# Splitting the second-layer weight sums and the activation split in two, and fetching the Wb tiles three steps ahead, in a fused attention and two-MoE kernel

## The chip, the cores and the metric

One core of a Trainium2 chip. The metric is the device time of one execution in microseconds. The kernel before has a median of 1530.12 us over 3 runs (1529.88 to 1532.5).

## The reference

Three stages follow one another; all tensors hold B = 8 batches of S = 576 tokens, 4608 tokens in all, and 512 model columns (8 heads of 64):

```python
p_packed = sm_attn(p, k, v)                  # 32 packed queries per head
x = sm_attn(q, p_packed, p_packed)           # then heads side by side: 4608 x 512
h = x @ w_in                                 # 512 x 2048
P = a[0] + a[1]*h + a[2]*h**2 + a[3]*h**3
Q = 1 + |b[0]|*|h| + |b[1]|*h**2
x = (P / (Q + 1e-6)) @ w_out                 # 2048 x 512
h = x @ moe2_w_in
out = (max(h, 0) + alpha*min(h, 0)) @ moe2_w_out
```

The weights come as 64-bit floats and are turned into 32-bit floats on the chip.

## The kernel before

**The three parts.** Until about 177 us the attention runs, and PE folds its second product with `w_in` into a matrix Wb for each batch (stored to DRAM, `wb_d`). From 177 to about 829 us the first MoE runs; it is the part in which the change lies. After that the second MoE runs as seven block products by sums of weight blocks (lines 1067 and 1075), which were made ready during the first MoE.

**The steps of the first MoE.** The loop at L843 takes 72 steps and three more (`LAG` = 3). Step g is one chunk c of 512 tokens and one f of the eight 256-column slices of the hidden layer. Nine chunks take pieces ("shares") of two batches' visits, 192 and 320 tokens, 256 and 256, or 320 and 192. In step g PE runs 24 matmuls of `emit_L1(g)` (L600: h = a2 times a Wb tile) and then 24 of `emit_L2(g - 3)` (L680: into `acc`). Each product is made of three passes over pairs of a high and a low half, which is why every operand is split: a copy rounded to the high half on ACT, and the rest by a subtraction on POOL. h lies in PSUM and has two buffers.

**The other engines in a step.** ACT: Abs (L642), two Identity (L643, L644), the high half of the activation of the step before (L626), the reciprocal square root (L657) and its square (L658). POOL: q times r (L645), the low half (L627). DVE: two operations on v (L650, L651) and three that end the step (L663 to L665, the last to read h). At f = 2 two finished accumulators go out through `yo` (L616, L614) and six stores (L621).

**The Wb tiles.** A visit is the use of one batch's Wb; `VISITS` lists ten, eight batches and two of them a second time. Tile n is visit n // 8, slice n % 8. It is first used at step n - 8, as the second share of a chunk, and again at step n. `next_wb(g)` at the end of step g first brings the tile fetched in the step before to its slot (`split_wb`): for a first visit ACT and POOL split it (L520, L521); for the second visits (tiles 48 to 55 and 72 to 79) the two halves, which `keep_wb` (L526) had stored, are read straight to the slot by one DMA (L518). Then it fetches tile g + 16 (`fetch_wb`, L511). So a tile is fetched 16 steps ahead of its number, and split or read back 15 ahead.

**The activations.** At f = 1 the next chunk's a2 is loaded (L495), and at f = 3, at the end of the step, `split_a2` splits it whole (L501 on ACT, L502 on POOL).

**The second layer's weights.** `w2_step(s, part)` is called at three places of a step ("start", "dve" and "end"); with n, half = divmod(s - 9, 2) it takes a 64-bit weight tile n through two steps. Its magnitude is made on ACT from the high words (L84) and the low words (L85), bounded on DVE (L89), joined (L92) and signed (L95). Each pair of tiles then yields four sums on POOL (L714), is stored by two DMAs (`w2_store`, L719), and its buffers, three in all under the tag `s4`, are loaded anew (`w2_load`, L707). So four steps make one cycle:

- n even, half 0 (f = 1 and 5): start: store the pair before, load tile n + 1; DVE: bound n;
- n even, half 1 (f = 2 and 6): DVE: join and sign n; end: magnitude of n + 1;
- n odd, half 0 (f = 3 and 7): start: load n + 1; DVE: bound n;
- n odd, half 1 (f = 4 and 0): DVE: join and sign n; end: magnitude of n + 1, and the four sums of the pair.

All DMAs named here are issued by SP, in the order of the program; one that waits keeps back those behind it.

Of the kernel before, what the change touches and what calls it, by code (L numbers as in the profile page):

```python
# [11 lines left out]
F32 = mybir.dt.float32  # L12
F32R = mybir.dt.float32r
I32 = mybir.dt.int32
I64 = mybir.dt.int64
U8 = mybir.dt.uint8
AF = mybir.ActivationFunctionType
ALU = mybir.AluOpType
# [10 lines left out]
def attention_then_two_moes(ctx, tc, qT, kT, v, pT, w_in, w_out, ab, w2_in, w2_out, alpha, out):  # L29
    nc = tc.nc  # L30
    mm = nc.tensor.matmul
    act = nc.scalar.activation
    dve = nc.vector
    pool = nc.gpsimd
# [7 lines left out]
    CH = 512  # L42
    NCH = NT // CH
    NF = 16
    NP = NF // 2
    LAST = B // 2 - 1
    VISITS = (0, 1, 2, 3, 4, 5, 0, 6, 7, 3)
# [31 lines left out]
    REBIAS = 2.0 ** -112  # L79
    HIGH_R = float(np.array(0x0FEFFFFF, np.int32).view(np.float32))  # L80

    def magnitude(w, st):
        words = st.bitcast(I32).rearrange("p (n t) -> p n t", t=2)
        act(w, words[:, :, 1].bitcast(F32), AF.Abs, scale=REBIAS)  # L84
        act(words[:, :, 0], st.bitcast(U8).rearrange("p (n t) -> p n t", t=8)[:, :, 3], AF.Copy, scale=1.0 / 32, bias=-31.0 / 64)  # L85
        return words

    def bounded(w):
        dve.tensor_scalar(w, w, 0.0, HIGH_R, op0=ALU.max, op1=ALU.min)  # L89
# [18 lines left out]
    def s2_tile():  # L108
        return gp.tile([128, 512], F32, tag="s2", name="s2", bufs=3)
# [99 lines left out]
    for h in range(4):  # L209
        o = 64 * (h % 2)  # L210
# [267 lines left out]
    spx = open_pool("spx", bufs=2, side="right")  # L478
    a2_t = {}

    chunks, taken = [], [0] * B
    for c in range(NCH):
        o, now = 0, []
        for i, n in enumerate(SHARES[c % 3]):
            b = VISITS[c + i]
# [9 lines left out]
            nc.sync.dma_start(out=st[:, :, o:o + n], in_=a2_d[b][:, :, t:t + n])  # L495
        a2_t[c] = st

    def split_a2(c):
        st = a2_t[c]
        t = spx.tile([128, 2, 2, CH], F32R, tag="a2t", name="a2t")  # L500
        act(t[:, 0], st, AF.Copy)  # L501
        pool.tensor_tensor(t[:, 1], st, t[:, 0], op=ALU.subtract)  # L502
        a2_t[c] = t

    def fetch_wb(n):
        v, f = divmod(n, NP)
        if v > VISITS.index(VISITS[v]):
            wb_q.append((v, f, None))
            return
        wb_q.append((v, f, s2_tile().rearrange("p (k f) -> p k f", k=2)))  # L510
        nc.sync.dma_start(out=wb_q[-1][2], in_=wb_d[VISITS[v]][:, 256 * f:256 * f + 256].rearrange("(k p) f -> p k f", p=128))  # L511
# [16 lines left out]
    w2_st, w2_mag = {}, {}  # L528

    def w2_abs(n):  # L530
        if n < 2 * NF:
            st = w2_st[n]
            if st.dtype == I64:
                w2_mag[n] = s2_tile()
                magnitude(w2_mag[n], st)
# [20 lines left out]
    for c in DRAIN.split():  # L556
        if c == "W":
            store_Wb()
            emit_Wb(nwb[0])
            nwb[0] += 1  # L560
        elif c == "L":
            load_a2(0)
        elif c == "l":
            split_a2(0)
        elif c == "o":
            load_late(len(late_st))
            w2_st[len(late_st) - 1 - LATE] = late_st[-1]
        elif c == "a":
            w2_abs(magged[0] - LATE)
            magged[0] += 1  # L570
        elif c == "c":
            w2_range(-LATE)
            w2_bits(-LATE)
        else:
            {"A": emit_a2, "B": store_a2, "S": emit_s2, "E": emit_exp2, "Q": load_q}[c[0]](NQ - int(c[1]))
# [8 lines left out]
    NG = NCH * NP  # L584
# [46 lines left out]
    def emit_E1(s):  # L631


        late_step(s, "start")
        w2_step(s, "start")
        if s < NG:
            h = hps.pop(s)
            r_ = spa.tile([128, 2, CH], F32, tag="r_", name="r_", bufs=1)
            q_ = spa.tile([128, 2, CH], F32, tag="q_", name="q_", bufs=2)
            v_ = vs[s] = spa.tile([128, 2, CH], F32, tag="v_", name="v_", bufs=2)  # L640
            now[s] = h, r_, q_, v_
            act(r_, h, AF.Abs)  # L642
            act(q_, r_, AF.Identity, scale=b1, bias=b0)  # L643
            act(v_, h, AF.Identity, scale=a3, bias=a2c)  # L644
            pool.tensor_tensor(q_, q_, r_, op=ALU.mult)  # L645
        if 1 <= s <= NG:
            emit_hi(s - 1)
        late_step(s, "middle")
        if s < NG:
            dve.tensor_tensor(v_, v_, h, op=ALU.mult)  # L650
            dve.scalar_tensor_tensor(v_, in0=v_, scalar=a1c, in1=h, op0=ALU.add, op1=ALU.mult)  # L651
# [47 lines left out]
    def w2_load(n):  # L699
        if n < 2 * NF:  # L700
            if n < 0:
                load_late(n + NF - EARLY)
                w2_st[n] = late_st[-1]
                return
            src, view = w2_source(n)
            st = w2_st[n] = gp.tile([128, 512 if src.dtype == I64 else 1024], src.dtype, tag="s4", name="s4", bufs=3)
            nc.sync.dma_start(out=view(st[:, 0:512]), in_=src)  # L707

    def w2_sums(n):

        a11, a22, s1, s2, s3, s4 = piece(n - 1, 0), piece(n, 1), piece(n - 1, 2), piece(n - 1, 3), piece(n, 2), piece(n, 3)
        a12, a21 = (piece(n - 1, 1), piece(n, 0))[::1 if n < NF else -1]
        for o, a, b, op in ((s1, a21, a22, ALU.add), (s3, a11, a21, ALU.subtract), (s2, s1, a11, ALU.subtract), (s4, a12, s2, ALU.subtract)):
            pool.tensor_tensor(o, a, b, op=op)  # L714

    def w2_store(n):
        y, r = divmod(n // 2, HF)
        for h in range(2):
            nc.sync.dma_start(out=wq_d[y][r // 2][:, 4 * h:4 * h + 4, r % 2, :],  # L719
                              in_=w2_st.pop(n - 1 + h).bitcast(F32).rearrange("p (i f) -> p i f", i=4))  # L720
# [23 lines left out]

    def w2_step(s, part):


        n, half = divmod(s - 9, 2)
        if part == "start" and not half:
            if n % 2 == 0 and 2 <= n <= 2 * NF:  # L750
                w2_store(n - 1)
            if n >= -1:
                w2_load(n + 1)
        elif part == "dve":
            if 0 <= n < 2 * NF:
                (w2_bits if half else w2_range)(n)
        elif part == "end" and half:
            if n >= -1:
                w2_abs(n + 1)
            if n % 2 and 0 <= n < 2 * NF:  # L760
                w2_sums(n)

# [47 lines left out]
    def split_y(s, i, src):  # L812
# [15 lines left out]
                dve.tensor_tensor(lo, x, hi, op=ALU.subtract)  # L828
        return rest

    def next_wb(g):

        while wb_q:
            split_wb()
        if g + 2 * NP < len(VISITS) * NP:
            fetch_wb(g + 2 * NP)
        c, f = divmod(g, NP)
        for i in range(3) if g == 0 else (g + 2,) if g + 2 < NP else ():
            keep_wb(0, i)
        if c == 2:  # L840
            keep_wb(3, f)

    for g in range(NG + LAG):  # L843
        if g == NG:
            close_pool("spx")
            spy = open_pool("spy", bufs=1, side="right")
            load_y(0)
        if g < NG:
            c, f = divmod(g, NP)
            if f == 1 and c + 1 < NCH:  # L850
                load_a2(c + 1)
            emit_L1(g)
            for _ in range(FILL[g] if g < len(FILL) else 0):
                emit_Wb(nwb[0])
                nwb[0] += 1
        if g == LAG - 1:
            close_pool("psw2")
            close_pool("psw")
            psa = open_pool("psa", bufs=1, space=PSUM, side="right")
        emit_E1(g)  # L860
        if g >= LAG:
            emit_L2(g - LAG)
        emit_E2(g)
        store_Wb()
        if g < NG:
            next_wb(g)
            if f == 3 and c + 1 < NCH:
                split_a2(c + 1)
        d = g - NG
        if d == -1:  # L870
            pool.tensor_scalar(nalpha, alpha_sb, -1.0, None, op0=ALU.mult)
            for n, st in enumerate((gp.tile([128, 2, CH], F32, tag="ast", name="wst", bufs=1),
                                    spa.tile([128, 2, CH], F32, tag="q_", name="wst", bufs=2))):
                for x in range(2):
                    w_load(2 * n + x, st[:, x])
        elif d >= 0:
            if d == 0:
                for n, tag in ((2, "v_"), (3, "q_")):
                    st = spa.tile([128, 2, CH], F32, tag=tag, name="wst", bufs=2)
                    for x in range(2):  # L880
                        w_load(2 * n + x, st[:, x])
            for u in range(4 * d, min(4 * d + 4, SOON)):
                w_split(u, dve)()
            if d:
                split_y(0, d - 1, y_block(0, d - 1, 0))()
# [155 lines left out]
    for u in range(len(units) + 2):  # L1041
        if u < len(units):
            s, y, i, n = units[u]
# [11 lines left out]
            w = ws.pop(u)  # L1055
# [6 lines left out]
            if y == 0:  # L1062
                for g in range(2):
                    q = 0
                    for x, z in PASSES:
                        for k in range(2):
                            mm(ps[:, g, 0:m], w[:, g, x, 128 * k:128 * k + 128], ysp[s, i](z, k),  # L1067
                               start=not onto and q == 0, stop=q == 5, skip_group_check=again)
                            q += 1
            else:  # L1070
                t = vsp.pop(u)
                for g in range(2):
                    for d in range(2):
                        for q, (x, z) in enumerate(PASSES):
                            mm(ps[:, d, 0:m], w[:, g, x, 128 * d:128 * d + 128], t[:, z, g, 0:m],  # L1075
                               start=not onto and n == 0 and g == 0 and q == 0, stop=n == 3 and g == 1 and q == 2,
# [61 lines left out]
```

## Time and profile before

| | |
|---|---|
| median of 3 runs | 1530.12 us |
| profiled execution | 1529.2 us, span 1527.4 us |
| PE busy | 1460.6 us (96%) |
| DVE busy | 1297.4 us (85%) |
| ACT busy | 1030.2 us (67%) |
| POOL busy | 570.4 us (37%) |

Shares are of the whole span. All times in rows are microseconds from the span's start, unless marked ns. A releaser in brackets (`[2.01 <-POOL q L645]`) is the idle time just before an instruction and what ended it. PE's matmuls are pipelined and their ends are modelled, so that the distance of two starts says more than a duration. The clock is the share of its full speed that TensorE was granted.

### The profile page before, as it was taken

The numbers are of one execution on the slowest core, as the hardware profiler recorded it, in microseconds if no ns is written. First come the engines' busy times: TensorE is split into PE (matmuls) and PEld (weight loads), VectorE is DVE, ScalarE is ACT, GpSimd is POOL, SyncE is SP. The second block draws the span as 40 slices with busy tenths as digits, with TensorE's granted clock in tenths as the row PEclk, the third lists the DMA queues.
The fourth block names the chain that finished last, engine by engine and source line by source line (L and its number), as shares of the span: only waits on it lengthen the run. The fifth ranks groups of instructions, "written<-read, shape, count | busy, mean of one in ns | idle before, by whom it ended". The sixth has DMA issues, their size and how long they took to land.

```text
span 1527.4 us, 20922 instructions
## 1 busy us (share of the span) xinstructions
PE 1460.6 (96%) x7712; PEld 1204.5 (79%) x7712; DVE 1297.4 (85%) x1412; ACT 1030.2 (67%) x1194; POOL 570.4 (37%) x354
## 2 busy tenths in 40 slices
PE   4798878999999999999999999999999999999998
PEld 2444477888888888888888877888888888888898
DVE  5988789898889999899999799859966996599586
ACT  4456588988988888888886586447434743474363
POOL 3132288788787778877664610000000000000000
PEclk9899989999999999999999999999999999999999
DMA  9999944236433632424435977997567656765694
GB/s 353 342 315 295 318 154 130 67 110 200 156 111 97 211 107 84 125 97 145 145 97 194 329 241 252 376 379 273 202 209 281 194 201 213 249 193 200 218 407 169
DMA packets 151109, 322.25 MB, mean 211 GB/s; under 512 B 14816, under 2 KB 79328, under 8 KB 149984
## 3 DMA queue, kind: packets, MB, share of 16 engines
q1 hardware_dynamic: 147552, 308.34, 59.1%
q0 software_dynamic: 2304, 8.39, 1.4%
q10 hardware_dynamic: 1152, 4.19, 0.8%
q8 instruction: 61, 1.00, 0.3%
q14 instruction: 40, 0.33, 0.1%
HBM read 230.17 MB, written 90.70 MB: 210 GB/s over the span
## 4 chain that ended last, share of the span: by engine, by line
PE 55%; DVE 13%; ACT 11%; POOL 5%; issue 4%; DMA 2%; SPq 0%; POOLq 0%; ACTq 0%; DVEq 0%
PE p L1075 21%; PE p L1067 20%; PE acc L680 8%; PE h L600 5%; DVE s L92 2%; POOL s L714 1%; DVE v L910 1%; ACT h L658 1%; DVE s L89 1%; DVE s L95 1%; POOL wb L521 1%; DVE v L927 1%; ACT wb L520 1%; DVE h L664 1%; PE pw L421 1%
## 5 line engine op out<-in xcount | busy, mean ns | idle before, releaser
L680 PE MATMUL acc<-gt,wo 128*128 128x512 f32 x1728 | 406.4, 391 | 6.7 <-ACT yo L616 6.7
L680 PEld LDWEIGHTS acc<-gt,wo 128*128 128x128 f32 x1728 | 320.2, 188 | 72.4 <-ACT yo L616 8.0
L1067 PE MATMUL p<-ysp,ws 128*128 128x512 f32 (+1 forms) x1680 | 346.9, 368 | 3.0 <-ACT vsp L995 2.4
L1075 PE MATMUL p<-vsp,ws 128*128 128x512 f32 (+1 forms) x1680 | 346.5, 368 | 0.2 <-DVE vsp L996 0.2
L1067 PEld LDWEIGHTS p<-ysp,ws 128*128 128x128 f32 x1680 | 292.5, 189 | 56.8 <-ACT vsp L995 3.4
L1075 PEld LDWEIGHTS p<-vsp,ws 128*128 128x128 f32 x1680 | 292.3, 189 | 53.7 <-DVE vsp L996 1.4
L600 PEld LDWEIGHTS h<-a2t,wb 128*128 128x128 f32 x1728 | 230.6, 193 | 27.5 <-issue 16.9
L600 PE MATMUL h<-a2t,wb 128*128 128x192 f32 (+2 forms) x1728 | 236.9, 294 | 14.9 <-DVE v__1857 L665 4.7
L995 ACT ACTIVATE vsp<-v 128x1024 fp32r<-128x1024 f32 (+1 forms) x140 | 135.7, 971 | 147.7 <-PE p L1075 98.3
L996 DVE TENSOR_TENSOR vsp<-v,vsp 128x1024 fp32r<-128x1024 f32 (+1 forms) x140 | 156.1, 1115 | 32.3 <-ACT vsp L995 31.8
L910 DVE TENSOR_TENSOR v<-v,p 128x1024 f32<-128x1024 f32 (+1 forms) x100 | 110.9, 1110 | 40.6 <-PE p L1067 40.4
L927 DVE SCALAR_TENSOR_TENSOR v<-r,nalpha,v 128x512 f32<-128x512 f32 (+1 forms) x160 | 112.4, 744 | 29.7 <-ACT v L922 29.7
L921 ACT ACTIVATE r<-v 128x1024 f32<-128x1024 f32 (+1 forms) x60 | 58.3, 972 | 76.1 <-DVE v L910 75.8
L910 DVE TENSOR_TENSOR v<-v 128x1024 f32<-128x1024 f32 (+1 forms) x80 | 88.7, 1113 | 0.0
L521 POOL TENSOR_TENSOR wb<-s,wb 128x512 fp32r<-128x512 f32 x48 | 64.2, 1339 | 31.9 <-ACT wb L520 31.7
L89 DVE TENSOR_SCALAR s<-s 128x512 f32<-128x512 f32 x48 | 61.8, 1288 | 1.1 <-ACT s L84 1.1
L922 ACT ACTIVATE v<-v 128x1024 f32<-128x1024 f32 (+1 forms) x60 | 58.6, 976 | 1.9
L421 PE MATMUL pw<-w_in,pph 128*128 128x512 f32 x96 | 51.0, 642 | 8.1 <-ACT wbs L433 7.4
L92 DVE SCALAR_TENSOR_TENSOR s<-s,s 128x512 int32<-128x512 int32 x40 | 56.7, 1418 | 0.4
L935 ACT ACTIVATE v<-p 128x1024 f32<-128x1024 f32 (+1 forms) x20 | 18.8, 942 | 53.3 <-PE p L1067 53.3
L910 DVE TENSOR_TENSOR c<-c,p 128x1024 f32<-128x1024 f32 (+1 forms) x25 | 27.4, 1112 | 29.9 <-PE p L1075 29.6
L369 POOL TENSOR_TENSOR trn<-trn,mx 128x576 f32<-128x576 f32 x16 | 19.5, 1217 | 73.2 <-DVE mx L368 67.7
(1026 smaller groups left out, 2236.6 us busy)
## 6 DMA issues: line engine op xcount, KB each, us to landing
ws<-wh_d SPq DMA_DIRECT2D x224, 512.0 KB, 5.6
wh_d<-ws SPq DMA_DIRECT2D x56, 512.0 KB, 4.9
wq_d<-s SPq DMA_DIRECT2D x32, 512.0 KB, 3.7
wst<-wq_d SPq DMA_DIRECT2D x56, 256.0 KB, 3.9
wb_d<-wbs SPq DMA_DIRECT2D x48, 256.0 KB, 5.2
s<-in_w_out SPq DMA_DIRECT2D x24, 512.0 KB, 4.3
s<-wb_d SPq DMA_DIRECT2D x48, 256.0 KB, 4.0
kt<-in_kT SPq DMA_DIRECT2D x16, 576.0 KB, 6.4
```

Source lines behind the costliest of these rows:

```text
L89: dve.tensor_scalar(w, w, 0.0, HIGH_R, op0=ALU.max, op1=ALU.min)
L92: dve.scalar_tensor_tensor(wi, in0=wi, scalar=3, in1=low, op0=ALU.logical_shift_left, op1=ALU.bitwise_or)
L421: mm(pw, pph[bp][:, j].rearrange("p a b -> p (a b)"), w_in_t[j, fc], start=True, stop=True)
L521: pool.tensor_tensor(t[:, 1], st, t[:, 0], op=ALU.subtract)
L600: mm(h[:, ft, o:o + m], w[x][:, k, 128 * ft:128 * ft + 128], a2_t[c][:, y, k, o:o + m], start=n == 0, stop=n == 5)
L680: mm(acc[d // 2][:, d % 2, :], w[:, x, 128 * d:128 * d + 128], t[:, y, ft, :], start=f == 0 and (x, y, ft) == (0, 0, 0), stop=f == NP - 1 ...
L910: dve.tensor_tensor(o, a, b, op=op)
L927: dve.scalar_tensor_tensor(v_[:, g], in0=r[:, g], scalar=nalpha[:, f:f + 1], in1=v_[:, g], op0=ALU.mult, op1=ALU.add)
L995: act(t[:, 0, :, 0:m], src, AF.Copy)
L996: return lambda: dve.tensor_tensor(t[:, 1, :, 0:m], src, t[:, 0, :, 0:m], op=ALU.subtract)
L1067: mm(ps[:, g, 0:m], w[:, g, x, 128 * k:128 * k + 128], ysp[s, i](z, k), start=not onto and q == 0, stop=q == 5, skip_group_check=again)
L1075: mm(ps[:, d, 0:m], w[:, g, x, 128 * d:128 * d + 128], t[:, z, g, 0:m], start=not onto and n == 0 and g == 0 and q == 0, stop=n == 3 and g ...
```

## The change

- The four sums of a pair are made in two parts: the first two (s1, s3) where all four were, at the end of the step with f = 4 or 0, the other two (s2, s4) in the middle of the next step (f = 1, 5), after that step's `emit_E1`.
- `w2_store` moves from the start to the end of that step; the load of tile n + 1 for even n moves there too, behind the store. For odd n the load stays where it is.
- The magnitude moves from the end of a step to the next one: the high words in the middle of the step, the low words at its end.
- `split_a2` works on one half of the rows at f = 3 and the other at f = 6, in the middle of these steps.
- Wb tiles are fetched 11 steps ahead of their number (`AHEAD`) instead of 16; they are split or read back one step later, as before. In steps 0 to 4 none is fetched.

```diff
+    def split_a2(c, ks):
+        if ks.start == 0:
+            a2_raw[c] = a2_t[c]
+            a2_t[c] = spx.tile([128, 2, 2, CH], F32R, tag="a2t", name="a2t")
+        t, st = a2_t[c], a2_raw[c]
+        act(t[:, 0, ks], st[:, ks], AF.Copy)
+        pool.tensor_tensor(t[:, 1, ks], st[:, ks], t[:, 0, ks], op=ALU.subtract)
...
-    def w2_sums(n):
+    def w2_sums(n, part):
...
-        for o, a, b, op in ((s1, ...), (s3, ...), (s2, ...), (s4, ...)):
+        for o, a, b, op in ((s1, ...), (s3, ...), (s2, ...), (s4, ...))[2 * part:2 * part + 2]:
             pool.tensor_tensor(o, a, b, op=op)
...
         n, half = divmod(s - 9, 2)
-        if part == "start" and not half:
-            if n % 2 == 0 and 2 <= n <= 2 * NF:
-                w2_store(n - 1)
-            if n >= -1:
-                w2_load(n + 1)
+        done = n - 1 if not half and n % 2 == 0 and 2 <= n <= 2 * NF else None
+        if part == "start" and not half and n % 2 and n >= -1:
+            w2_load(n + 1)
+        elif part == "middle":
+            if done:
+                w2_sums(done, 1)
+            if not half and 0 <= n < 2 * NF and w2_st[n].dtype == I64:
+                w2_mag[n] = s2_tile()
+                high_word(w2_mag[n], w2_st[n])
         elif part == "dve":
             if 0 <= n < 2 * NF:
                 (w2_bits if half else w2_range)(n)
-        elif part == "end" and half:
-            if n >= -1:
-                w2_abs(n + 1)
-            if n % 2 and 0 <= n < 2 * NF:
-                w2_sums(n)
+        elif part == "end":
+            if half and n % 2 and 0 <= n < 2 * NF:
+                w2_sums(n, 0)
+            elif not half and 0 <= n <= 2 * NF:
+                if n < 2 * NF and w2_st[n].dtype == I64:
+                    low_word(w2_st[n])
+                if done:
+                    w2_store(done)
+                if n % 2 == 0:
+                    w2_load(n + 1)
...
+    AHEAD = NP + 3
...
-        if g + 2 * NP < len(VISITS) * NP:
-            fetch_wb(g + 2 * NP)
+        if 2 * NP <= g + AHEAD < len(VISITS) * NP:
+            fetch_wb(g + AHEAD)
...
         emit_E1(g)
+        if g < NG and f in (3, 6) and c + 1 < NCH:
+            split_a2(c + 1, slice(f // 6, f // 6 + 1))
+        w2_step(g, "middle")
         if g >= LAG:
             emit_L2(g - LAG)
...
             next_wb(g)
-            if f == 3 and c + 1 < NCH:
-                split_a2(c + 1)
```

The two lines of `magnitude` become functions of their own, `high_word` and `low_word`, and the first chunk's split names both halves at once.

## Rows read from the trace of the kernel before

**Rows 1.** Windows: stretch, its length, each engine's busy time, granted clock, DMA share, GB/s

```profile
829.00:1527.00 698.00, 691.34 (x3358) 584.34 (x3358) 554.83 (x595) 368.52 (x416) 32.28 (x20) 1.00 0.72 255
```

**Rows 2.** Timelines of PE, ACT and POOL, steps 41 to 43

```profile
552.17 3.25 PE L600 MATMUL h<-a2t,wb 128*128 128x320 f32 x24
...
560.76 3.25 PE L600 MATMUL h<-a2t,wb 128*128 128x320 f32 x24
...
546.94 1.03 ACT L642 ACTIVATE r__5041<-h 128x1024 f32<-128x1024 f32 x1 [0.32 <-PE h L600]
...
555.52 1.03 ACT L642 ACTIVATE r__5113<-h 128x1024 f32<-128x1024 f32 x1 [0.46 <-PE h L600]
...
560.27 2.42 POOL L627 TENSOR_TENSOR gt<-v__5043,gt 128x1024 fp32r<-128x1024 f32 x1
```

**Rows 3.** Timeline of PE: the first L600 of steps 24 and 32

```profile
395.88 3.34 PE L600 MATMUL h<-a2t,wb 128*128 128x192 f32 x24
...
466.25 3.09 PE L600 MATMUL h<-a2t,wb 128*128 128x256 f32 x24
```

**Rows 4.** The page's groups of instructions: the matmuls of both products

```profile
L680 PE MATMUL acc<-gt,wo 128*128 128x512 f32 x1728 | 406.4, 391 | 6.7 <-ACT yo L616 6.7
...
L600 PE MATMUL h<-a2t,wb 128*128 128x192 f32 (+2 forms) x1728 | 236.9, 294 | 14.9 <-DVE v__1857 L665 4.7
```

**Rows 5.** Timeline of ACT, steps 20 to 24

```profile
365.47 1.01 ACT L642 ACTIVATE r__3406<-h 128x1024 f32<-128x1024 f32 x1
...
372.92 0.66 ACT L84 ACTIVATE s<-s 128x512 f32<-128x512 f32 x1
...
381.06 1.15 ACT L657 ACTIVATE r__3491<-q__3492,qc 128x1024 f32<-128x1024 f32 x1 [2.01 <-POOL q__3492 L645]
...
383.74 1.01 ACT L642 ACTIVATE r__3564<-h 128x1024 f32<-128x1024 f32 x1
...
399.96 1.01 ACT L642 ACTIVATE r__3716<-h 128x1024 f32<-128x1024 f32 x1
```

**Rows 6.** Timelines of POOL and DVE, steps 19 to 21

```profile
365.95 2.41 POOL L502 TENSOR_TENSOR a2t<-ast,a2t 128x1024 fp32r<-128x1024 f32 x1
...
374.45 0.74 POOL L714 TENSOR_TENSOR s<-s 128x256 f32<-128x256 f32 x1 [1.36 <-DVE s L95]
...
371.33 2.31 DVE L92 SCALAR_TENSOR_TENSOR s<-s,s 128x512 int32<-128x512 int32 x1
```

**Rows 7.** Timeline of POOL: L645 of step 4, right behind L502

```profile
223.04 2.40 POOL L645 TENSOR_TENSOR q__2131<-q__2131,r__2130 128x1024 f32<-128x1024 f32 x1
```

**Rows 8.** Timeline of SP, step 41: start and length of each issue

```profile
549.09 1.19 SPq L719 DMA_DIRECT2D wq_d<-s  x2
552.10 0.35 SPq L707 DMA_DIRECT2D s<-in_w_out  x1
552.50 0.45 SPq L511 DMA_DIRECT2D s<-wb_d  x1
```

**Rows 9.** L518's transfers: landing of all sixteen, of one at 519.2, one at 529.0

```profile
DMA to landing us min/median/max: 3.2/5.7/7.5
...
L518 SPq DMA_DIRECT2D wb<-wbh_d x1: 515/515/515, 519.2 to 519.2; - x1
...
DMA to landing us min/median/max: 5.3/5.3/5.3
...
L518 SPq DMA_DIRECT2D wb<-wbh_d x1: 320/320/320, 529.0 to 529.0; - x1
...
DMA to landing us min/median/max: 3.2/3.2/3.2
```

**Rows 10.** Timeline of PE after two waits, and the window of the first

```profile
234.26 4.92 PE L600 MATMUL h<-a2t,wb 128*128 128x192 f32 x24 [2.16 <-DVE v__2132 L665]
...
905.48 2.97 PE L1067 MATMUL p<-ysp,ws 128*128 128x512 f32 x12 [2.41 <-ACT vsp L995]
...
234.20:239.00 4.80, 4.74 (x24) 4.77 (x25) 4.70 (x5) 4.39 (x6) 3.48 (x3) 0.64 0.19 77
```

More of the change, by code (lines that the diff above doesn't have):

```diff
@@ L80, in attention_then_two_moes, with high_word, low_word, magnitude @@
     HIGH_R = float(np.array(0x0FEFFFFF, np.int32).view(np.float32))
-    def magnitude(w, st):
+    def high_word(w, st):
+        act(w, st.bitcast(F32).rearrange("p (n t) -> p n t", t=2)[:, :, 1], AF.Abs, scale=REBIAS)
+    def low_word(st):
         words = st.bitcast(I32).rearrange("p (n t) -> p n t", t=2)
-        act(w, words[:, :, 1].bitcast(F32), AF.Abs, scale=REBIAS)
         act(words[:, :, 0], st.bitcast(U8).rearrange("p (n t) -> p n t", t=8)[:, :, 3], AF.Copy, scale=1.0 / 32, bias=-31.0 / 64)
         return words
+    def magnitude(w, st):
+        high_word(w, st)
+        return low_word(st)
     def bounded(w):
@@ L496, in load_a2 @@
         a2_t[c] = st
[L498 to L503, printed above, removed]
+    a2_raw = {}
+    def split_a2(c, ks):
[5 more added lines that the diff above has]
+        pool.tensor_tensor(t[:, 1, ks], st[:, ks], t[:, 0, ks], op=ALU.subtract)
     def fetch_wb(n):
@@ L563, in attention_then_two_moes @@
         elif c == "l":
-            split_a2(0)
+            split_a2(0, slice(0, 2))
         elif c == "o":
@@ L707, in w2_load @@
             nc.sync.dma_start(out=view(st[:, 0:512]), in_=src)
-    def w2_sums(n):
+    def w2_sums(n, part):
         a11, a22, s1, s2, s3, s4 = piece(n - 1, 0), piece(n, 1), piece(n - 1, 2), piece(n - 1, 3), piece(n, 2), piece(n, 3)
         a12, a21 = (piece(n - 1, 1), piece(n, 0))[::1 if n < NF else -1]
-        for o, a, b, op in ((s1, a21, a22, ALU.add), (s3, a11, a21, ALU.subtract), (s2, s1, a11, ALU.subtract), (s4, a12, s2, ALU.subtract)):
+        for o, a, b, op in ((s1, a21, a22, ALU.add), (s3, a11, a21, ALU.subtract), (s2, s1, a11, ALU.subtract), (s4, a12, s2, ALU.subtract))[2 * part:2 * part + 2]:
             pool.tensor_tensor(o, a, b, op=op)
```

## The prediction

> **What bounds the kernel now.** I read the page's groups first, then windows by stage, then the timelines of the five engines over one chunk (eight steps), and last the issues of SP, the one queue that nearly all transfers go through, and their landings. From 829 us on PE is busy 691.34 of 698 us [rows 1], and no edit reaches that part, so the whole effect lies in the steps before it. There a step is 24 matmuls of L600 and 24 of L680; where nothing disturbs it, L600 starts every 8.59 us (552.17, 560.76) [rows 2], 68.7 for a chunk with shares 192 and 320. Chunk 3 takes 466.25 - 395.88 = 70.37 us [rows 3]: PE is not the limit there, but the loop through ACT, POOL and DVE, since h has two buffers and L600 of step g waits for L665 of step g-2. What PE loses to the others in all these steps is bounded by the page: 6.7 us before L680 (on yo) and 14.9 before L600, of which 4.7 on L665 [rows 4]. So a chain made shorter can hardly bring more than 12 us (6.7 + 4.7), and a late weight tile has no such ceiling.
>
> I call the four steps in which a pair of w2 tiles is made A, B, C, D (A is f = 1 and 5, D is f = 0 and 4). By the starts of L642, D and A at f 4, 5 take 383.74 - 365.47 = 18.27 us, B and C at f 6, 7 take 399.96 - 383.74 = 16.22 [rows 5]; f 0 to 3 take the other 35.9 of the chunk.
>
> **Part 1, the chain (sums, magnitudes, a2).** In A, L657 waits 2.01 us for POOL's L645 [rows 5], because the sums, 0.74 us for one [rows 6], run on POOL ahead of it, all four. Two of them move behind L627: 1.5 us earlier. L84 (0.66 us [rows 5]) now stands ahead of L657 in A and C, mostly inside the half microsecond of wait that stays: +0.2. That is -1.3 for f 4, 5, and by the same layout -0.9 for f 0, 1, whose D has no L502 beside it. The a2 split leaves the end of f 3, where ACT spends 1 us on L501 and POOL 2.41 on L502 [rows 6]; half of it comes back in f 3, giving about -0.65 for f 2, 3. The other half goes to f 6: 0.5 us on ACT, and 1.2 on POOL between L627 and L521, beside which DVE's integer steps stretch (the L92 that ran beside POOL's L627 took 2.31 us [rows 6]), so that L95, then L665, then the next L626 come later: +1.3. With 0.2 for L84 in C, f 6, 7 get 2.0 longer. Sum per chunk -1.3 - 0.9 - 0.65 + 2.0 = -0.85, say -0.9; over the three and a half chunks in which both kernels split tiles and the loop decides, -3.1. Splits are now 10 steps ahead of a tile's number instead of 15, so that ACT and POOL carry L520 and L521 in some ten steps (33 to 37 and 57 to 61) that had none: +1.3. At the start, step 3 no longer ends with all of L502, for which POOL's L645 had to wait until 223.04 [rows 7]: -1.0; but two halves at steps 3 and 6 each push DVE's words, and the words of one tile move a step: together -0.7 (between -2 and +1.5). Net **-2.5**, bounds -6 and +1.
>
> Edits that I cost at nothing: the moved fetches (L511) no longer stand for L95 on SP, which carries no work that anyone waits for at that time, their tiles being split a step later; a split tile is complete on POOL, by the layout, some 11.6 us after the Abs (L642) of its step, against 13.8 (546.94 to 560.76 [rows 2]) until the L600 that wants it. That cover is thin, some 2 us; where L511 lands late, L520 holds up ACT, at most 0.65 per chunk.
>
> **Part 2, the re-read tiles.** Sixteen tiles (numbers 48 to 55 and 72 to 79) are not split but read back whole by L518, 512 KB each. A tile of number n is first used at step n - 8. Its DMA was issued seven steps ahead of that; now it is at the end of step n - 10, two ahead, and behind all that SP issues in that step. In B, C and D little stands there. In A, SP first issues w2_store (L719), which waits for POOL's second pair of sums, then w2_load (L707), whose buffer is free only when the first store has landed, and only then L518. So it is four tiles that count, at steps 41, 45, 65 and 69. With the Abs of A at 0:
> - POOL's L627 ends at 560.27 + 2.42 - 555.52 = 7.2 [rows 2]; the first sum of the pair takes 0.75 and some 0.3 beside DVE's L89: 8.3. The first store is issued then.
> - Store to load took 552.10 - 549.09 = 3.0 [rows 8], the landing of the store. The next DMA follows at 552.50, 0.4 later: 8.3 + 3.0 + 0.4 = 11.7 or 11.8 for L518.
> - L518 lands in 5.3 us where it stood behind a load (the one at 519.2), in 3.2 where it stood alone (529.0), over all sixteen in 3.2 to 7.5, median 5.7 [rows 9]. I take 5.3, since here it is behind the load again: 17.1.
> - L600 of A + 2 starts at 560.76 - 546.94 = 13.8 after the Abs of A [rows 2], and needs the new tile only for its second share, a quarter of 3.25 us later: 14.6.
>
> PE stands 17.1 - 14.6 = 2.5 us, four times: **+10.0**. At these steps nothing is split any more, PE is the limit, and a wait of it is not made up. The bounds are 0.4 each with a landing of 3.2, and 4.7 with one of 7.5; between them I stay near 5.3 to 5.7. The L518 in B of f 2 (steps 42, 66) has six y_d stores ahead and would be late too; the wait of the step before gives it the room, so no term.
>
> The clock adds to that. After PE had stood 2.16 us before 234.26, its 24 matmuls took 4.92 us instead of some 3.3, at a granted clock of 0.64 [rows 10]; 2.41 us before 905.48 changed nothing, 12 matmuls in 2.97 [rows 10]. One of two: half of 1.6 us, four times, **+3.3** (bounds 0 and 6.6). What decides between the two rows the trace doesn't show.
>
> Sum: 10.0 + 3.3 - 2.5 = +10.8 on the profiled run of 1529.2, that is 1540.0; the median of the runs is 1530.12, so I forecast 1541.
>
> The Trainium skill, "DMA: Bandwidth & Descriptors", section "Anatomy of one DMA — SWDGE (gpsimd) path", gives a transfer some 2.0 us plus its bytes by 436 GB/s, fitted on GpSimd's queue; by it 512 KB take 3.2 us, an estimate. The lone L518 agrees with it (3.2), the one behind a load doesn't (5.3) [rows 9]. By the page's figure alone the sum would be that of the first rival below.
>
> **Rivals.**
> *The tile comes in time.* If L518 lands as the one alone did, 3.2, it is there at 11.8 + 3.2 = 15.0, PE stands 0.4 each, 1.6 in all, and the clock stays: 1.6 - 2.5 = -0.9, **1529**. For it: no L511 is issued in these steps any more, so less is under way. Against it: 3.2 is the least of sixteen, and here the load of 512 KB goes just ahead. Chance 0.15.
> *Faster.* The half of L502 in f 6 finds POOL and DVE free and costs 0.5 rather than 2.0, so that the loop falls under PE's pace. It decides where B and C of f 6, 7 take under 17.2 us, twice 8.59. A chunk then runs at the floor: 68.7 - 70.4 = -1.7, three and a half times -6.0; the +1.3 goes, the -0.7 stays, and with the tile in time (1.6) the sum is -5.1: **1525**. For it: PE's waits of 6.7 and 4.7 [rows 4] are there to be had. Against it: 16.22 [rows 5] leaves one microsecond, and half of L502 alone takes 1.2 on POOL. Chance 0.15.
> *Slower still.* Landings of 6.3, between 5.3 and 7.5 [rows 9], give 3.5 each, and the low clock each time 1.6: 4 x (3.5 + 1.6) - 2.5 = +17.9, **1548**. This is the upper end of my own case.
>
> **How the numbers follow.** 0.2% is 3.1 us, about what a measurement of this kernel can tell from no change. The forecast case has 0.70; its own range is 1533 to 1548. The first rival lies within 0.2%, the second below. So faster 0.15, same 0.15, slower 0.70. The range that holds 8 in 10 reaches from the first rival's lower side, 1527, to 1548.
>
> **What would show it.** In the trace after: PE standing before L600 for "DMA wb<-wbh_d" at steps 43, 47, 67 and 71, some 2.5 us each, and after some of these a granted clock under 1; on SP, at steps 41, 45, 65 and 69, L719, then L707 some 3 us later, then L518; L714 in two pairs per cycle with L657's wait in A down from 2.01 to about 0.5; L502 in halves of some 1.2 us; a chunk with splits at about 69.5 instead of 70.4; SP's long wait for L95 gone. The forecast is wrong if L518 lands in 4 us or less there, if the store goes out before 8 us after the Abs, or if PE is so far behind at these steps that it asks later.

## The result and the profile after

The changed kernel took 1539.03 us (median of 6 runs, 1534.95 to 1541.63) against 1530.0 us (1528.9 to 1533.1): a ratio of 1.0052, 95% interval 1.0032 to 1.0071. It is slower, by some 8 to 9 us. The profiled execution was the shortest of the six, 1534.95 us with a span of 1532.8.

In the changed kernel's line numbers L600 is L609, L680 is L689, L518 is L527, L707 is L716, L719 is L728, L642 is L651, L657 is L666 and L665 is L674.

The page's groups of the two products, to be held against [rows 4] (the last column is PE's idle time before the group and what ended most of it):

```profile
L689 PE MATMUL acc<-gt,wo 128*128 128x512 f32 x1728 | 406.5, 391 | 3.7 <-ACT yo L625 3.7
...
L609 PE MATMUL h<-a2t,wb 128*128 128x192 f32 (+2 forms) x1728 | 238.2, 295 | 23.8 <-DMA wb<-wbh_d 9.2
```

PE stands 3.0 us less for yo, and before L609 there is a wait that was not there before: 9.2 us for tiles read back from `wbh_d`. The view of waits gives their number and the longest (in total, times, longest):

```profile
PE h L609 <- DMA wb<-wbh_d: 9.2, 4, 2.6
```

The timeline of PE has them at steps 43, 47, 67 and 71. A step's L609 is cut in two there, six matmuls of the first share (the row at 556.31), and 18 after the wait:

```profile
556.31 1.06 PE L609 MATMUL h<-a2t,wb 128*128 128x320 f32 x6
559.92 2.46 PE L609 MATMUL h<-a2t,wb 128*128 128x192 f32 x18 [2.55 <-DMA wb<-wbh_d]
...
596.40 4.05 PE L609 MATMUL h<-a2t,wb 128*128 128x192 f32 x18 [1.89 <-DMA wb<-wbh_d]
...
772.13 2.48 PE L609 MATMUL h<-a2t,wb 128*128 128x192 f32 x18 [2.40 <-DMA wb<-wbh_d]
...
809.07 2.47 PE L609 MATMUL h<-a2t,wb 128*128 128x192 f32 x18 [2.33 <-DMA wb<-wbh_d]
```

Behind the second of the four, 18 matmuls took 4.05 us, behind the others 2.46 to 2.48. The windows over the second and the first of these groups show the granted clock (third number from the end of the line), 0.56 against 1.00, that is mostly 1.2 GHz against 2.4:

```profile
596.40:600.30 3.90, 3.90 (x19) 3.90 (x19) 3.87 (x4) 0.63 (x1) 1.92 (x2) 0.56 0.52 201
559.90:562.20 2.30, 2.28 (x18) 2.28 (x19) 2.27 (x3) 0.00 (x0) 0.00 (x0) 1.00 0.93 294
```

SP's timeline in step 41 answers to [rows 8]; the step's Abs is the row of ACT below it:

```profile
551.18 1.20 SPq L728 DMA_DIRECT2D wq_d<-s  x2
554.19 0.35 SPq L716 DMA_DIRECT2D s<-in_w_out  x1
554.63 0.40 SPq L527 DMA_DIRECT2D wb<-wbh_d  x1
...
542.49 1.03 ACT L651 ACTIVATE r__5030<-h 128x1024 f32<-128x1024 f32 x1 [0.79 <-PE h L609]
```

From the Abs the store goes out after 8.7 us, the load 3.0 later, the tile's DMA 0.4 after that, at 12.1; PE resumes at 559.92, 17.4 after the Abs.

Against that, the loop through ACT, POOL and DVE became shorter. Chunk 3, 70.37 us in [rows 3], is 462.23 - 392.73 = 69.50 now:

```profile
392.73 3.34 PE L609 MATMUL h<-a2t,wb 128*128 128x192 f32 x24
...
462.23 3.04 PE L609 MATMUL h<-a2t,wb 128*128 128x256 f32 x24
```

So the two profiles differ by +9.2 for the waits, +1.6 for the matmuls at the low clock, and some -5.4 for all the rest, which makes the 5.4 us between their spans (0.9 of the -5.4 lies ahead of the first step, in code that the change doesn't touch).

### The profile page after: what moved, and what is told of

It is laid out like the page before. It is cut to its first block, busy times and chain, and to the rows that moved or that the text cites. A ratio compares the mean times of both kernels' runs of the same rounds, so it can differ in the third digit from the quotient of the medians.

```text
span 1532.8 us, 20960 instructions
## 1 busy us (share of the span) xinstructions
PE 1461.3 (95%) x7712; PEld 1208.3 (79%) x7712; DVE 1308.4 (85%) x1412; ACT 1029.4 (67%) x1202; POOL 577.0 (38%) x362
## 4 chain that ended last, share of the span: by engine, by line
PE 48%; DVE 18%; ACT 14%; issue 4%; DMA 4%; POOL 4%; SPq 1%; DVEq 0%; ACTq 0%; POOLq 0%
PE p L1095 23%; PE p L1087 21%; DVE s L98 3%; PE h L609 2%; DVE s L101 2%; DVE h L673 2%; PE acc L689 2%; ACT h L667 2%; ACT gt L635 1%; DMA wb<-wbh_d 1%; POOL gt L636 1%; ACT s L83 1%; DVE s L95 1%; DMA wq_d<-s 1%; DVE v L947 1%
## 5 line engine op out<-in xcount | busy, mean ns | idle before, releaser
L689 PE MATMUL acc<-gt,wo 128*128 128x512 f32 x1728 | 406.5, 391 | 3.7 <-ACT yo L625 3.7
L689 PEld LDWEIGHTS acc<-gt,wo 128*128 128x128 f32 x1728 | 320.4, 188 | 69.2 <-ACT yo L625 4.7
L609 PE MATMUL h<-a2t,wb 128*128 128x192 f32 (+2 forms) x1728 | 238.2, 295 | 23.8 <-DMA wb<-wbh_d 9.2
L609 PEld LDWEIGHTS h<-a2t,wb 128*128 128x128 f32 x1728 | 232.2, 194 | 35.0 <-issue 16.7
L95 DVE TENSOR_SCALAR s<-s 128x512 f32<-128x512 f32 x48 | 67.0, 1396 | 0.9 <-ACT s L83 0.9
```

Source lines behind the costliest of these rows:

```text
L609: mm(h[:, ft, o:o + m], w[x][:, k, 128 * ft:128 * ft + 128], a2_t[c][:, y, k, o:o + m], start=n == 0, stop=n == 5)
L689: mm(acc[d // 2][:, d % 2, :], w[:, x, 128 * d:128 * d + 128], t[:, y, ft, :], start=f == 0 and (x, y, ft) == (0, 0, 0), stop=f == NP - 1 ...
```

## The experiments

All were timed against runs of the kernel before on the same chip, 1529 to 1530 us in median. The first four ask what makes the tiles late and what the change is worth without that.

**Only the later fetch**, in the kernel before:

```diff
-        if g + 2 * NP < len(VISITS) * NP:
-            fetch_wb(g + 2 * NP)
+        if 2 * NP <= g + NP + 3 < len(VISITS) * NP:
+            fetch_wb(g + NP + 3)
```

> The kernel before with the later fetch alone (11 steps ahead of a tile's number instead of 16; sums, magnitudes, store, load and a2 as before). My theory, that four re-read tiles are late because their DMA stands behind the store and the load at the end of a step A: here store and load go out at the start of A and are some 9 us ahead, so PE does not stand for a tile at steps 43, 47, 67 and 71; the re-read behind the y_d stores of steps 42 and 66 may cost up to 1 us each. 1530 to 1533 us, no or nearly no wait of L600 for a wbh_d tile. The rival, that two steps ahead of use is too late whatever stands before it on SP: the four waits of some 2.3 us are there again, 1538 or more.

1534.05 us (1530.24 to 1535.96), ratio 1.0019 (1.0008 to 1.0029). The four waits are not there. In step 41 SP has the tile's DMA out at 551.16, 5.9 us after the step's Abs and not 12.1, behind a store issued at the start of A, and nothing waits for it. What is left is two waits at steps 44 and 68, in sum 1.2 us, where the DMA stands behind the six stores of yo:

```profile
551.16 0.40 SPq L518 DMA_DIRECT2D wb<-wbh_d  x1
561.94 3.04 SPq L621 DMA_DIRECT2D y_d<-yo  x6
565.07 0.44 SPq L518 DMA_DIRECT2D wb<-wbh_d  x1
...
569.00 2.47 PE L600 MATMUL h<-a2t,wb 128*128 128x192 f32 x18 [0.25 <-DMA wb<-wbh_d]
```

The distance alone is thus not what costs 9 us. The median lies a little above what was expected, and 4.2 us above that of the kernel before. Part of it is in the profile: chunks 4 and 7, where five more steps split a tile than in the kernel before, take 70.37 us each instead of 68.75 and 68.70 (by the starts of L600). The profiled run (1530.73) is one of the shorter ones, so that what the longer runs had is not shown.

**The changed kernel with the far fetch:**

```diff
-    AHEAD = NP + 3
+    AHEAD = 2 * NP
```

> The changed kernel with the old distance of the fetches (16), all else as changed. My theory: the four waits of 9.2 us in sum and what the clock takes behind them go, and what the shorter chain gives stays; by the profile of the changed kernel, which at step 40 was 4.5 us ahead of the one before, that leaves about 1524 (1522 to 1527), 0.3 to 0.5% below the kernel before. The rival, that the later split of the tiles (not the sums and the a2 halves) is what made the chain shorter: 1529 to 1531.

1523.65 us (1521.87 to 1524.45), ratio 0.9956 (0.9944 to 0.9969): no wait for a tile, and 0.44% below the kernel before. The gain of the chain doesn't hang on the later splits.

**Distance 11, but the tile's DMA ahead of store and load:**

```diff
             emit_L2(g - LAG)
+        if wb_q and wb_q[0][2] is None:
+            split_wb()
         emit_E2(g)
```

> The changed kernel, distance 11 kept, with only the order on SP changed: a re-read tile's DMA is issued right after the matmuls of the step are emitted, ahead of this step's store and load, so a few us earlier in the same step. My theory (the place behind the store): no wait of L600 for a tile, 1524 to 1527, like the far fetch. The rival (too late in any place): waits of 1 to 2 us remain, 1533 or more.

1523.05 us (1520.65 to 1524.49), ratio 0.9954 (0.9941 to 0.9966), no wait for a tile. The time it gains is larger than the few microseconds that I expected. The DMA of step 41 is now the one at 527.84, more than 20 us before the store:

```profile
527.84 0.59 SPq L527 DMA_DIRECT2D wb<-wbh_d  x1
551.54 1.19 SPq L728 DMA_DIRECT2D wq_d<-s  x2
```

SP is far ahead of the other engines and then stands at the store until POOL has the sums. In the changed kernel it stands there 265.8 us in 32 waits, up to 24.3 at a time (in total, times, longest), and all that it could have issued in that time stands behind:

```profile
SPq L728 <- POOL s L723: 265.8, 32, 24.3
```

**The DMA between store and load** splits the blame of these two:

```diff
                 if n % 2 == 0:
+                    if wb_q and wb_q[0][2] is None:
+                        split_wb()
                     w2_load(n + 1)
```

> The changed kernel with the re-read tile's DMA between the store and the load of step A, instead of behind both. My theory, that the load's wait for the landing of the store (3 us) is what makes the tile late: the DMA goes out some 9 us after the Abs instead of 11.8, lands at about 14.5, and PE stands 0 to 0.5 us: 1523 to 1525. The rival, that the wait for POOL's sums ahead of the store is as bad: waits of 1 us and more remain, 1527 or more.

1526.09 us (1524.39 to 1528.92), ratio 0.9980 (0.9970 to 0.9990). Four waits are left, 1.5 us in sum and 0.5 at most. The DMA goes out at 553.17, and the tile is there when PE resumes at 558.59:

```profile
551.88 1.20 SPq L728 DMA_DIRECT2D wq_d<-s  x2
553.17 0.74 SPq L527 DMA_DIRECT2D wb<-wbh_d  x1
...
558.59 2.46 PE L609 MATMUL h<-a2t,wb 128*128 128x192 f32 x18 [0.50 <-DMA wb<-wbh_d]
```

So the load's wait for the store to land makes most of the lateness, as I held, but the wait for the sums alone uses up the slack too: the second store waits for the last sum, and the DMA went out 1.3 us after the first store, not 0.4. The median lies between the two expectations, 2.4 us above that of the far fetch; the profile's waits make 1.5 of it.

**Everything one step sooner:**

```diff
-    AHEAD = NP + 3
+    AHEAD = NP + 4
```

> The changed kernel with every fetch one step sooner (12 steps ahead of a tile's number). The re-read DMA keeps its place behind store and load but has 8.6 us more. My theory: no wait of L600 for a tile, and the chain's gain stays whole: 1522 to 1525. The rival, that the place in step A costs in itself (transfers that stretch one another): 1528 or more.

1522.87 us (1521.88 to 1524.09), ratio 0.9958 (0.9944 to 0.9972), no wait for a tile. With one step more the place behind store and load does no harm.

The next ones ask where the chain's gain comes from.

**The far fetch with a2 split whole**, at the end of f = 3 as before:

```diff
...
-        if g < NG and f in (3, 6) and c + 1 < NCH:
-            split_a2(c + 1, slice(f // 6, f // 6 + 1))
...
             next_wb(g)
+            if f == 3 and c + 1 < NCH:
+                split_a2(c + 1, slice(0, 2))
```

> The far fetch with the a2 split whole again, at the end of f = 3, so that only sums, magnitudes, store and load are changed against the kernel before. By the prediction's layout the two halves cost 1.3 to 1.4 us a chunk and this is faster than the far fetch by 2 to 4 us, about 1521. The rival, that the halves are what gives the gain in the chain: slower than the far fetch by 2 to 5 us, 1526 to 1529.

1521.37 us (1520.25 to 1524.02), ratio 0.9952 (0.9939 to 0.9966). The interval covers that of the far fetch: the difference of 2.3 us in the medians has the sign that I expected and isn't told from none.

**Only the a2 halves**, in the kernel before (with `split_a2` as in the change):

```diff
...
         emit_E1(g)
+        if g < NG and f in (3, 6) and c + 1 < NCH:
+            split_a2(c + 1, slice(f // 6, f // 6 + 1))
...
-            if f == 3 and c + 1 < NCH:
-                split_a2(c + 1)
```

> The kernel before with only the a2 split in two halves, in the middle of f = 3 and f = 6. By the prediction's layout that costs 2.0 us at f = 6 and gives 0.65 at f = 3 for a chunk whose loop decides: slower by 2 to 5 us in all, 1532 to 1535. The rival, that POOL and DVE have the room: within 1 us of the kernel before, or faster.

1529.08 us (1526.51 to 1532.49), ratio 0.9999 (0.9990 to 1.0007): nothing. My expectation fell, the rival's stands.

**Only the magnitudes**, in the kernel before:

```diff
...
+        elif part == "middle":
+            if not half and 0 <= n < 2 * NF and w2_st[n].dtype == I64:
+                w2_mag[n] = s2_tile()
+                high_word(w2_mag[n], w2_st[n])
...
-        elif part == "end" and half:
-            if n >= -1:
-                w2_abs(n + 1)
-            if n % 2 and 0 <= n < 2 * NF:
+        elif part == "end":
+            if not half and 0 <= n < 2 * NF and w2_st[n].dtype == I64:
+                low_word(w2_st[n])
+            if half and n % 2 and 0 <= n < 2 * NF:
                 w2_sums(n)
...
         emit_E1(g)
+        w2_step(g, "middle")
```

> The kernel before with only the magnitudes moved: the high words to the middle of a step, the low words to its end. In A the high words should fall into the 2 us in which L657 waits for POOL, so that a cycle is about 0.6 us shorter: over the chunks that the loop decides some 4 us, 1526 (1524 to 1528). The rival, that the gain of the changed kernel's chain comes from the sums: 1529 to 1531.

1540.34 us (1539.15 to 1544.29), ratio 1.0076 (1.0063 to 1.0088): slower by 0.8%, and neither expectation held. The timeline of ACT in B and C of f 6, 7 (steps 22 and 23) of this kernel, in which L648 is the line of L642, L632 that of L626, L663 that of L657, L671 that of L665, and L83 and L87 make the magnitude:

```profile
384.84 1.01 ACT L648 ACTIVATE r__3564<-h 128x1024 f32<-128x1024 f32 x1
...
392.37 1.01 ACT L648 ACTIVATE r__3640<-h 128x1024 f32<-128x1024 f32 x1
...
398.01 1.06 ACT L632 ACTIVATE gt<-v__3566 128x1024 fp32r<-128x1024 f32 x1 [2.26 <-DVE v__3566 L671]
398.98 0.65 ACT L83 ACTIVATE s<-s 128x512 f32<-128x512 f32 x1
399.53 1.14 ACT L663 ACTIVATE r__3640<-q__3641,qc 128x1024 f32<-128x1024 f32 x1
...
401.67 0.66 ACT L87 ACTIVATE s<-s 128x512 int32<-128x512 uint8 x1
...
402.75 1.01 ACT L648 ACTIVATE r__3716<-h 128x1024 f32<-128x1024 f32 x1
```

B and C take 402.75 - 384.84 = 17.91 us, 1.7 more than the 16.22 of [rows 5]. With no magnitude at its end B is over sooner on ACT, in 7.53 us, but that gains nothing: in C ACT waits 2.26 us for the L665 of B, which DVE has to give first, and C takes 10.38 us. That L665 also comes later, and the wait ends 13.2 us after B's Abs. In the kernel before there was no wait, and L626 of C started 12.0 us after B's Abs (395.76). DVE and POOL show where this 1.1 to 1.2 us comes from, the kernel before first, then this one (L101 is the line of L95, L527 that of L521):

```profile
391.45 0.69 DVE L95 SCALAR_TENSOR_TENSOR s<-s,s 128x512 int32<-128x512 int32 x1
392.58 1.30 POOL L521 TENSOR_TENSOR wb<-s,wb 128x512 fp32r<-128x512 f32 x1 [1.72 <-ACT wb L520]
```

```profile
392.55 1.83 DVE L101 SCALAR_TENSOR_TENSOR s<-s,s 128x512 int32<-128x512 int32 x1
392.54 1.30 POOL L527 TENSOR_TENSOR wb<-s,wb 128x512 fp32r<-128x512 f32 x1 [0.57 <-ACT wb L526]
```

Before, with the magnitude ahead of the split on ACT at the end of B, POOL's part of the split began when DVE was through with L95. Without it that part runs beside the DVE instruction, which takes 1.83 us instead of 0.69. The remaining 0.56 us is L87 at the end of C (401.67 to the next start on ACT, at 402.23); L83 costs next to nothing there, since L657 had 0.46 us of wait in its place before. This is one pair of steps; the others were not followed in this way.

**Only the sums, with store and load**, in the kernel before (magnitudes and a2 as they were):

```diff
...
-        if part == "start" and not half:
-            if n % 2 == 0 and 2 <= n <= 2 * NF:
-                w2_store(n - 1)
-            if n >= -1:
-                w2_load(n + 1)
+        done = n - 1 if not half and n % 2 == 0 and 2 <= n <= 2 * NF else None
+        if part == "start" and not half and n % 2 and n >= -1:
+            w2_load(n + 1)
+        elif part == "middle":
+            if done:
+                w2_sums(done, 1)
...
         elif part == "end" and half:
             if n >= -1:
                 w2_abs(n + 1)
             if n % 2 and 0 <= n < 2 * NF:
-                w2_sums(n)
+                w2_sums(n, 0)
+        elif part == "end":
+            if done:
+                w2_store(done)
+            if n % 2 == 0 and 0 <= n <= 2 * NF:
+                w2_load(n + 1)
...
         emit_E1(g)
+        w2_step(g, "middle")
```

> The kernel before with only the sums in two parts, and with them the store and the load of the even step at its end. L657 no longer waits 2 us in A, which gives 1.5 us a cycle on the loop; but the load now lands some 17 us after the Abs of A, when the magnitude at the end of B wants the tile: if it is late, ACT stands there and takes the gain back. My theory: it is in time by a little, 1525 to 1528. The rival, that the load is late by a microsecond or two in each cycle: 1531 to 1536.

1522.0 us (1520.4 to 1526.37), ratio 0.9957 (0.9943 to 0.9971): the whole gain. The wait of 2.01 us before L657 [rows 5] is down to 0.49; the load is late once in a while by up to 1.1 us, as the rival had it, but the loop takes that:

```profile
378.00 1.16 ACT L657 ACTIVATE r__3485<-q__3486,qc 128x1024 f32<-128x1024 f32 x1 [0.49 <-POOL q__3486 L645]
...
388.99 0.67 ACT L84 ACTIVATE s<-s 128x512 f32<-128x512 f32 x1 [1.08 <-DMA s<-in_w_in]
```

**The changed kernel once more:**

> The changed kernel as it is, profiled in another execution, to see why its runs lie 7 us apart (1534.95 to 1541.63). My theory: the four waits for a re-read tile stay at 2 to 2.6 us each, 9 to 10 us in all, and what differs is behind how many of them the clock is low, 1.6 us for one: an execution some 3 to 5 us longer shows two to four such places against one in the first profile. The rival: the waits themselves differ, 12 us and more in a longer run, with the clock low behind one of them as before.

1537.48 us (1531.73 to 1545.0, 10 runs), ratio 1.0052 (1.0036 to 1.0068), like the first time. The profiled execution took 1539.85, 4.9 us longer than the first, and neither expectation explains that. The four waits are 8.0 us (9.2 in the first), and two of them (not one) have the low clock behind them, which together leaves the steps as long as in the first profile. The difference lies ahead of the first step (it starts at 181.83 instead of 176.56), in code that the change doesn't touch: 2.5 us of it are there at the row at 174.78 (172.29 in the first profile), where PE had waited 2.24 us instead of 0.66, and of the rest 2.2 us are 6 matmuls that took 5.07 us instead of 2.84. The first fence is the second execution, with a window; the second is the first.

```profile
174.78 1.87 PE L427 MATMUL pw<-w_in,pph 128*128 128x512 f32 x2 [2.24 <-DVE wbs L437]
177.33 5.07 PE L427 MATMUL pw<-w_in,pph 128*128 128x512 f32 x6 [0.69 <-ACT wbs L439]
...
178.00:182.00 4.00, 4.00 (x7) 1.58 (x5) 2.40 (x4) 1.24 (x3) 0.00 (x0) 0.52 0.96 373
...
563.93 4.05 PE L609 MATMUL h<-a2t,wb 128*128 128x192 f32 x18 [1.99 <-DMA wb<-wbh_d]
...
601.99 2.48 PE L609 MATMUL h<-a2t,wb 128*128 128x192 f32 x18 [1.87 <-DMA wb<-wbh_d]
...
775.92 3.96 PE L609 MATMUL h<-a2t,wb 128*128 128x192 f32 x18 [2.18 <-DMA wb<-wbh_d]
```

```profile
172.29 1.13 PE L427 MATMUL pw<-w_in,pph 128*128 128x512 f32 x2 [0.66 <-DVE wbs L437]
174.28 2.84 PE L427 MATMUL pw<-w_in,pph 128*128 128x512 f32 x6 [0.87 <-ACT wbs L439]
```

## Why the prediction was right, and where not

**The tiles.** +10.0 was forecast and 9.2 came, by the steps as they were laid out: store 8.3 after the Abs (8.7 measured), load 3.0 later (3.0), the DMA at 11.8 (12.1), landed and used at 17.1 (17.4), 2.5 us of wait (2.55, 1.89, 2.40, 2.33). Three experiments settle the cause: the same distance without the waiting store and load in front has no such wait (the later fetch alone, and the DMA ahead of store and load), and the same place with one step more has none either. The choice between the landings was the step that mattered: the row behind a load (5.3 [rows 9]) was the right neighbour, since the four late tiles were used 5.2 to 5.3 us after their issue; the lone one (3.2) would have given 0.4 each. The Trainium skill's figure ("DMA: Bandwidth & Descriptors", section "Anatomy of one DMA — SWDGE (gpsimd) path", some 3.2 us for these bytes, an estimate) doesn't fit these transfers, 4.3 to 7.6 in the first profile of the changed kernel. What I overlooked is that SP has long been standing at the store: the tile could have gone out more than 20 us sooner, not a few.

**The clock.** One wait in two was taken to bring the low clock, +3.3. In the two profiles of the changed kernel it was 3 of 8, 1.5 to 1.6 us each, so 1.6 and 3.1 in all. Its price was right. Its rate is not contradicted, but eight waits are too few to fix one.

**The chain.** Forecast -2.5, or -3.8 without its +1.3 for the later splits; with the far fetch, which has neither the late tiles nor the later splits, the same kernel is 0.44% below the one before, -6.2 us in the medians. The mechanism was right, and its sizes in the pairs of steps nearly so. In chunk 2, by the starts of L651 held against L642 of [rows 5], f 4, 5 take 379.59 - 362.70 = 16.89 us, 1.4 less (forecast 1.3), and f 6, 7 take 397.35 - 379.59 = 17.76, 1.5 more (forecast 2.0):

```profile
362.70 1.00 ACT L651 ACTIVATE r__3385<-h 128x1024 f32<-128x1024 f32 x1
...
379.59 1.01 ACT L651 ACTIVATE r__3543<-h 128x1024 f32<-128x1024 f32 x1
...
397.35 1.00 ACT L651 ACTIVATE r__3697<-h 128x1024 f32<-128x1024 f32 x1
```

Chunk 3 is 0.87 shorter, as forecast, but chunks 1 and 6 are 1.60 and 1.66 shorter, so that chunks 1, 2, 3 and 6 gave 4.8 us (0.62 in chunk 2, by the starts of L600 and L609) where 3.1 stood for three and a half of them. What the sum lacked is a term for the chunks in which it held PE to be the limit. PE's 6.7 us of waits for yo [rows 4] stood in the prediction as a bound and in one rival, and in the sum at nothing. They are 3.7 in the changed kernel and 2.0 with the far fetch. Chunk 4, in which neither the kernel before nor the one with the far fetch splits a tile after its first step, shows it. It takes 535.00 - 466.25 = 68.75 us before and 530.84 - 463.35 = 67.49 with the far fetch, and of these 1.26 us the wait for yo makes 0.99 (chunk 7: 68.70 and 67.47). The first fence is the kernel before, the second the far fetch:

```profile
495.99 5.73 PE L680 MATMUL acc<-gt,wo 128*128 128x512 f32 x24 [1.33 <-ACT yo L616]
...
535.00 3.25 PE L600 MATMUL h<-a2t,wb 128*128 128x320 f32 x24
```

```profile
463.35 3.04 PE L609 MATMUL h<-a2t,wb 128*128 128x256 f32 x24
...
491.81 5.75 PE L689 MATMUL acc<-gt,wo 128*128 128x512 f32 x24 [0.34 <-ACT yo L625]
...
530.84 3.25 PE L609 MATMUL h<-a2t,wb 128*128 128x320 f32 x24
```

The "+1.3" for the splits in ten more steps did come, though the medians (0.9956 far, 0.9954 and 0.9958 with most or all of them) are too coarse to show it: at distance 11 with the tile's DMA ahead of store and load, chunk 4 takes 530.86 - 462.59 = 68.27 us, 0.8 more than with the far fetch, and chunk 7 as much more, 1.6 in all. In the changed kernel the two effects leave chunk 4 at 530.49 - 462.23 = 68.26, half a microsecond below the kernel before and not above it.

```profile
462.59 3.04 PE L609 MATMUL h<-a2t,wb 128*128 128x256 f32 x24
...
530.86 3.32 PE L609 MATMUL h<-a2t,wb 128*128 128x320 f32 x24
```

```profile
530.49 3.31 PE L609 MATMUL h<-a2t,wb 128*128 128x320 f32 x24
```

(The first of these is the kernel with the DMA ahead of store and load, the second the changed kernel.)

The bound of 12 us was misread in one part: the 4.7 on L665 is a single wait, at step 2, and it is 4.7 in the changed kernel too.

Of the edits, the sums alone give the whole gain (-0.43%). The a2 half in f 6 was priced too high: with the far fetch, f 6, 7 of chunk 3 take 17.77 us with the halves and 16.80 with a2 whole, 1.0 instead of 1.8, and f 2 to 5 are 0.8 shorter with them, so that nothing is left, as the run with the halves alone (0.9999) has it. And L84 and L85, which I had moved for almost nothing, were not free: alone +0.76%, and hidden only where the sums have moved too. Had the tiles been in time, this kernel would have come out at the time of the "faster" rival (1525) and not of the first (1529), but not by that rival's condition: B and C of f 6, 7 did not fall under 17.2 us.

**In sum**, 1541 was forecast and 1539 came, and two errors of opposite sign are in it. By the medians, each of them good to one or two microseconds, the chain gave 6.2 us instead of 3.8, and the late tiles together with the later splits cost, between the changed kernel and the one with the far fetch, 15.4 (1539.03 - 1523.65) instead of 14.6 (10.0, 3.3 and 1.3). That the sum lies so near is luck in part. The profile, the shortest of its six runs, shows 10.8 of the 15.4 in waits and low clock, and some 1.6 are the later splits.

**What remains open:** why the runs of the changed kernel lie so far apart (1531.73 to 1545.0), and with them the 3 us of the 15.4 that the profile doesn't show. The low clock behind some of the waits is shown in two executions and the late first step in one; that they make the whole spread isn't. That ACT, reaching f 2 sooner in the shorter chain, is why PE waits less for yo fits the rows but was not tested by itself.

## The better version

Five kernels are below both, by 0.42 to 0.48% of the kernel before, with intervals that overlap: the change with the far fetch (with a2 in halves or whole), with one step more, with the tile's DMA ahead of the store, and the kernel before with the sums alone in two parts (1522.0). The last is the smallest edit.

## What to carry to other kernels

A prefetch distance counted in steps says little: count in microseconds when its DMA can leave the queue, by what waits in front of it on the same queue, and give a transfer that is needed soon its place ahead of any store that waits for an engine. When work is moved along a loop, ask of each stretch which engine sets the pace there, and what will then run beside what: the magnitudes, moved alone, cost 0.8%, in the steps that were followed mostly because a split on POOL came to run beside DVE's integer work. A wait that is named as a bound wants a term in the sum too, or a reason for none. And two edits that go together should be priced together, since each can be the cover of the other.

## What the runs showed that I had not expected

The clock falls or stays after waits of like length: 4.05 us for the 18 matmuls behind waits of 1.89 and 1.99, 3.96 behind 2.18, but 2.46 to 2.48 behind 1.87, 1.95, 2.33, 2.40 and 2.55, at a granted clock of 0.56 and 1.00 in the windows read. In the range seen the wait's length doesn't decide it. POOL's L512, half of a2, took 1.76 us and not the half of 2.41 when DVE worked on words beside it:

```profile
386.69 1.76 POOL L512 TENSOR_TENSOR a2t<-ast,a2t 128x512 fp32r<-128x512 f32 x1
```
